# Two interleaved output chains in a seven-product down projection, block sums one per piece, earlier weight sums, and late stores and transposes on another queue

## The chip, the cores and the metric

The kernel runs on one core of a Trainium2 chip. The time is the device time of one launch in microseconds (us). Lower is better. Before the change it is 247.21 us, the median of three runs (245.82 to 247.61).

## The reference

The inputs are q, k and v of shape 4 x 8 x 768 x 64 (batch, heads, sequence, head width). A retention over time feeds a mixer: a low-rank product along the sequence, then a two-layer MLP with relu along the model width of 512 (hidden width 2048, rank 32).

```python
state = gamma * state + einsum('bhd,bhe->bhde', k[:, :, t], v[:, :, t])
y[:, :, t] = scale * einsum('bhd,bhde->bhe', q[:, :, t], state)   # for t = 0 .. 767
x = y.transpose(0, 2, 1, 3).reshape(4, 768, 512)
h = x.transpose(0, 2, 1) @ U @ V                                  # U 768 x 32, V 32 x 768
u = x + h.transpose(0, 2, 1)
out = u + maximum(u @ w_ch1, 0) @ w_ch2
```

## The kernel before

**Tiling.** The four batch elements are called blocks. A block's 768 rows are six chunks of 128. The recurrence is computed by chunks: `score` multiplies a chunk's k and q to 128 x 128 squares per head and VectorE multiplies these by the decay mask (tiles `a`, line 435); `mix` multiplies them with v and adds what the running state gives (bank `o`, line 450), and ScalarE copies the sum to `x`; `state` carries the state on. The low-rank product follows when a block has all six chunks: `lr_proj` (tile `pc`), `lr_expand` with four adds on VectorE into `x` (line 482), and then the transposed copy `uT`, in three pairs of chunks, by TensorE with a copy (`lr_turn_pe`) or by a transposing DMA (`lr_turn`, line 496).

**The MLP of a block.** The up projection is 32 pieces, each with four matmuls into an `mlp` bank: 16 of 512 columns and 16 of 256. A relu takes each bank into `gT`; every third one is on VectorE (line 629), the others are on ScalarE (line 631). Block 0's down projection is direct: 24 pieces of four matmuls. That of blocks 1 to 3 is Strassen's method with Winograd's sums. The 768 rows, the 2048 hidden units and the 512 columns are each cut in halves, and seven products of half-size blocks replace eight. Each product (p1 to p7) is made for three row tiles i of 128 rows, so there are 21 of them, each with eight matmuls of 256 columns. Before them stand sums on VectorE: of the weights, once (`w2_sums`, line 527, tiles `w2t`, four groups of four), and of the hidden values (`g_sums`, lines 535 to 538, tiles `gS`, and one in place in `gT`, four groups of four for each block). Behind them, VectorE takes the banks out: `keep` (line 565: `da` after p1, `db` after p6, `dc` after p7) adds the residual and keeps an intermediate result, `give` (line 571) adds it to the final half row. For one row tile, p1, p6, p7 and p4 are added up in one bank of the ring `A`, with a `keep` between them, p5 and p3 in bank `C`, and p2 is in bank `B`. A product that adds to a bank waits until the `keep` of the product before it in that bank is done, since both use the same bank.

**Stages.** `weave` runs the MLP of one block, with the retention and the low-rank product of the next block set in between at given shares of the MLP's length (the numbers in the tracks at the program's end). Stage k is the MLP of block k with the retention of block k+1; stage 3 has none. Startup and block 0's retention come ahead. In stage 0 and for most of stage 1, GpSimd (POOL) casts and scales what is loaded (line 263).

**What sets the order.** The schedule is manual: instructions are issued in program order, each engine works its own queue in that order, and an instruction waits on semaphores for its inputs and for its buffers. PSUM has eight banks, given out by rings (`RINGS`): `mlp` 0 to 2, `s` 3 and 4, `o` 5, `qk` 6, `st` 7; `A`, `B` and `C` of the down projection share 0, 6, 1 and 2 with these. DMAs are issued on ScalarE's queue (ACT: transposes, stores of blocks 1 to 3) and on SyncE's (SP: loads, block 0's stores).

## Time and profile before

| | |
|---|---|
| median of the runs | 247.21 us |
| the profiled execution: its time | 247.24 us |
| its span in the trace | 245.5 us |
| its mean granted TensorE clock | 0.993 of full speed |
| busy share of TensorE, VectorE, ScalarE, GpSimd | 89%, 60%, 36%, 34% |

The span is what the trace covers; the 1.7 us between it and the time lie around the program. The chain of work that ended last is mostly the seven products, and TensorE's time is mostly the up projection (columns: line, engine, operation, output and inputs, count, then busy time, mean of one in ns, then the idle time just ahead of these and what ended most of it):

```profile
PE 7%; DVE 0%; issue 0%
PE A L552 4%; PE C L552 2%; PE B L552 1%; DVE dc L565 0%; DVE o L571 0%; DVE da L565 0%
...
L624 PE MATMUL mlp<-uT,w1b 128*128 128x512 f16 (+1 forms) x512 | 90.6, 330 | 3.7 <-ACT gT L631 1.3
L435 DVE TENSOR_TENSOR a<-s,mask 128x512 bf16<-128x512 f32 x36 | 23.0, 681 | 7.4 <-PE s L431 7.4
L552 PE MATMUL A<-w2t,gT 128*128 128x256 f16 x144 | 18.6, 272 | 3.0 <-DVE dc L565 1.5
L450 PE MATMUL o<-vd,a 128*128 128x64 bf16 x144 | 8.2, 195 | 5.1 <-DVE a L435 5.0
L552 PE MATMUL A<-w2t,gS 128*128 128x256 f16 x72 | 9.3, 273 | 3.6 <-DVE da L565 3.6
```

The chain is followed back only as far as the trace releases it. The last number of a row says for how long TensorE stood still right ahead of those instructions, and for whom. Names are those of the program, with the buffer's number left out.

### The profile page before, as it was taken

How to read it: one execution, taken by the hardware profiler on the slowest of the kernel's cores; microseconds unless marked ns; L12 is line 12 of the kernel's file. 1: busy time of each engine (PE TensorE's matmuls, PEld its weight loads, DVE VectorE, ACT ScalarE, POOL GpSimd, SP SyncE). 2: the span in 40 equal slices, each digit the busy share in tenths (PEclk: the TensorE clock that was granted, in tenths of full speed). 3: DMA queues.
4: the chain of work that ended last, by engine and by line, in shares of the span. 5: the costliest groups of instructions: out<-in, count | busy, mean ns of one | idle time of the engine just before them, and what ended most of it. 6: DMA issues, size and time to landing. Idle time of an engine off the chain costs nothing. (4 is left out here: it accounts for less than half of the span.)

```text
span 245.5 us, 5333 instructions
## 1 busy us (share of the span) xinstructions
PE 218.7 (89%) x2149; PEld 144.4 (59%) x2152; DVE 146.7 (60%) x289; ACT 87.7 (36%) x175; POOL 83.5 (34%) x121
## 2 busy tenths in 40 slices
PE   7898999999999589967879979999799989998993
PEld 3466444866454335543668663665688745656882
DVE  6676444329796542786475664496955652757442
ACT  3267454554642155634311001665321014541000
POOL 5532988787887571465416100000000000000000
PEclk9999999999999999999799999999999999999999
DMA  6997999999999999999993154422222262000222
GB/s 186 294 288 181 324 328 275 375 268 220 220 195 234 232 240 176 224 189 231 206 166 116 45 128 132 86 47 43 43 45 88 98 158 45 0 0 4 85 85 88
DMA packets 94633, 39.22 MB, mean 160 GB/s; under 512 B 78096, under 2 KB 87312, under 8 KB 94608
## 3 DMA queue, kind: packets, MB, share of 16 engines
q1 hardware_dynamic: 73008, 29.43, 52.0%
q10 hardware_dynamic: 21600, 9.44, 16.3%
q8 instruction: 17, 0.28, 0.5%
q14 instruction: 8, 0.07, 0.1%
HBM read 27.85 MB, written 6.29 MB: 139 GB/s over the span
## 5 line engine op out<-in xcount | busy, mean ns | idle before, releaser
L624 PE MATMUL mlp<-uT,w1b 128*128 128x512 f16 (+1 forms) x512 | 90.6, 330 | 3.7 <-ACT gT L631 1.3
L624 PEld LDWEIGHTS <-w1b 128*128 128x128 f16 x512 | 48.8, 99 | 36.3 <-issue 5.1
L631 ACT ACTIVATE gT<-mlp 128x512 f16<-128x512 f32 (+1 forms) x88 | 43.2, 497 | 63.7 <-PE mlp L624 41.2
L629 DVE TENSOR_SCALAR gT<-mlp 128x256 f16<-128x256 f32 (+1 forms) x40 | 21.4, 536 | 36.9 <-PE mlp L624 36.7
L552 PEld LDWEIGHTS <-gT 128*128 128x128 f16 x288 | 27.5, 98 | 8.2 <-issue 4.6
L435 DVE TENSOR_TENSOR a<-s,mask 128x512 bf16<-128x512 f32 x36 | 23.0, 681 | 7.4 <-PE s L431 7.4
L84 ACT ACTIVATE x<-o 128x512 f16<-128x512 f32 x21 | 12.5, 596 | 37.0 <-PE o L450 24.3
L552 PEld LDWEIGHTS <-gS 128*128 128x128 f16 x216 | 20.6, 98 | 6.7 <-issue 3.9
L659 PE MATMUL mlp<-w2b,gT 128*128 128x512 f16 x96 | 24.2, 380 | 0.0
L263 POOL TENSOR_TENSOR qkd<-in,gq 128x512 bf16<-128x512 f32 x18 | 19.1, 1059 | 13.2 <-DMA in<-in_q_dram 10.2
L263 POOL TENSOR_TENSOR qkd<-in,gk 128x512 bf16<-128x512 f32 x18 | 19.5, 1084 | 8.5 <-DMA in<-in_k_dram 7.9
L552 PE MATMUL A<-w2t,gT 128*128 128x256 f16 x144 | 18.6, 272 | 3.0 <-DVE dc L565 1.5
L84 ACT ACTIVATE state<-st 64x256 bf16<-64x256 f32 x40 | 15.0, 375 | 7.0 <-PE st L328 3.8
L261 POOL CAST vd<-in 128x512 bf16<-128x512 f32 x18 | 11.9, 662 | 15.5 <-issue 9.6
L450 PE MATMUL o<-vd,a 128*128 128x64 bf16 x144 | 8.2, 195 | 5.1 <-DVE a L435 5.0
L552 PE MATMUL A<-w2t,gS 128*128 128x256 f16 x72 | 9.3, 273 | 3.6 <-DVE da L565 3.6
L659 PEld LDWEIGHTS <-gT 128*128 128x128 f16 x96 | 8.2, 98 | 7.2
L177 PE MATMUL mlp<-ones 128*128 128x512 bf16 x32 | 10.2, 448 | 1.8 <-DVE ones L170 1.4
L482 DVE TENSOR_TENSOR x<-s,x 128x256 f16<-128x256 f32 (+1 forms) x16 | 8.2, 552 | 5.8 <-PE qk L478 4.7
L565 DVE TENSOR_TENSOR dc<-A,x 128x256 f32<-128x256 f32 x9 | 3.8, 425 | 11.9 <-PE A L552 11.9
L290 POOL CAST w2b<-in 128x512 f16<-128x512 f32 x16 | 9.8, 613 | 2.3 <-DMA in<-in_moe_w_ch_dram 1.7
L450 PEld LDWEIGHTS <-a 128*128 128x128 bf16 x144 | 6.2, 99 | 6.9 <-DVE a L435 6.4
(110 smaller groups left out, 272.6 us busy)
## 6 DMA issues: line engine op xcount, KB each, us to landing
in<-in_moe_w_ch_dram SPq DMA_DIRECT2D x32, 256.0 KB, 5.7
in<-in_k_dram SPq DMA_DIRECT2D x24, 256.0 KB, 5.3
in<-in_q_dram SPq DMA_DIRECT2D x24, 256.0 KB, 5.5
in<-in_v_dram SPq DMA_DIRECT2D x24, 256.0 KB, 5.4
out_dram<-o ACTq DMA_DIRECT2D x18, 256.0 KB, 2.0
out_dram<-o SPq DMA_DIRECT2D x12, 128.0 KB, 3.7
Vf<-in_moe_V_dram SPq DMA_DIRECT2D x4, 96.0 KB, 4.0
qkT<-qkd ACTq DMA_TRANSPOSE x12, 3.1
```

What stands on the lines that cost most here:

```text
L84: nc.scalar.activation(dst, src, AF.Copy)
L177: nc.tensor.matmul(idle_bank[0], ones[:, :P], ones, start=True, stop=True, skip_group_check=True)
L261: nc.gpsimd.tensor_copy(out=t, in_=src)
L263: nc.gpsimd.tensor_tensor(t, src, g[:, ci, :, None].to_broadcast([P, H, D]), op=ALU.mult)
L290: nc.gpsimd.tensor_copy(out=w2b[:, m], in_=take("w2", m))
L435: nc.vector.tensor_tensor(a, four(sp[i]), causal(mask), op=ALU.mult)
L450: nc.tensor.matmul(o_p[:, ts(h, D)], a[i][:, h // 2], vb[:, h], start=(ci == 0 and h == 0), stop=True, skip_group_check=True)
L552: nc.tensor.matmul(acc[key, i], lhs[:, m, ts(i, P)], rhs[:, m], start=(fresh and m == 0), stop=(m == NH - 1), skip_group_check=True)
L624: nc.tensor.matmul(g_p[:, :sz], w1b[:, c, ts(m, P)], uTs[b][:, ds(j, nj), c], start=(c == 0), stop=(c == NCB - 1))
L629: nc.vector.tensor_relu(gT[:, m, ds(lo, sz)], g_p[:, :sz])
L631: nc.scalar.activation(gT[:, m, ds(lo, sz)], g_p[:, :sz], AF.Relu)
L659: nc.tensor.matmul(ch, gT[:, m, ts(j, P)], w2b[:, m], start=(m == 0), stop=(m == NM - 1))
```

## The change

It has six parts.

1. The 21 products come in a new order. Two row tiles' chains in the ring `A` are begun together: p1, p6 and p7 of tile 0 and tile 1 stand side by side, and other products lie between two of the same chain. The `give` of the lower right quarter now follows whichever of p5 and p7 is later. The intermediate tiles `d` and the masked scores `a` have two buffers each.
2. `g_sums` gives back its four sums as four steps, and these are hung one by one on four pieces in a row (from pieces 12, 16 and 24). Of the last group, two stand behind the last piece of the up projection, one behind p1 of tile 0 and one behind p1 of tile 1.
3. In blocks 1 to 3 every fourth relu is on VectorE, not every third.
4. From stage 1 on, the ring `mlp` has a fourth bank, number 6; the last expansion of the low-rank product takes bank `st` and the transposes on TensorE in stage 1 take bank `o`, both instead of `qk`.
5. The weight sums `w2_sums` stand earlier in stage 0: at 0.47, 0.52, 0.57 and 0.62 of its MLP instead of 0.58, 0.68, 0.78 and 0.88.
6. The stores of the MLP of blocks 2 and 3 and the transposes of block 3 (`qkT` and `uT`) are issued by SyncE instead of ScalarE.

```diff
-             "A": [0, 6], "B": [1], "C": [2]}
+             "A": [6, 0], "B": [1], "C": [2]}
...
     def turn_dma(b, ci):
-        nc.scalar.dma_start_transpose(
+        (nc.sync if b > 2 else nc.scalar).dma_start_transpose(
...
-            a = rmid.tile([P, 4, P], bf16, tag=f"a{i}", name=f"a{i}_{b}_{ci}")
+            a = rmid.tile([P, 4, P], bf16, tag=f"a{i}", bufs=2,
+                          name=f"a{i}_{b}_{ci}")
...
     def lr_turn(b, j):
-        nc.scalar.dma_start_transpose(
+        (nc.sync if b > 2 else nc.scalar).dma_start_transpose(
...
     def g_sums(gT, gS, m):
-        nc.vector.tensor_tensor(s1, a21, a22, op=ALU.add)
-        nc.vector.tensor_tensor(s2, s1, a11, op=ALU.subtract)
-        nc.vector.tensor_tensor(a21, a11, a21, op=ALU.subtract)
-        nc.vector.tensor_tensor(s4, a12, s2, op=ALU.subtract)
+        return [part(nc.vector.tensor_tensor, *x) for x in (
+            (s1, a21, a22, ALU.add), (s2, s1, a11, ALU.subtract),
+            (a21, a11, a21, ALU.subtract), (s4, a12, s2, ALU.subtract))]
...
-            t = outp.tile([P, DQ], fp32, tag=f"d{nm}", bufs=1,
+            t = outp.tile([P, DQ], fp32, tag=f"d{nm}", bufs=2,
...
-                stores.append((nc.scalar, out[b, ts(j, P)], r[0]))
+                stores.append((nc.sync if b > 1 else nc.scalar,
+                               out[b, ts(j, P)], r[0]))
...
+        def c22(i, nm):
+            done.add((nm, i))
+            if ("p5", i) in done and ("p7", i) in done:
+                give("C", i, i + NP, 1, held["c", i])
...
-            order += [(p1, i)] if i == 0 else []
-            order += [(p2, i), (p6, i), (p5, i), (p7, i)]
-            order += [(p1, i + 1)] if i + 1 < NP else []
-            order += [(p4, i), (p3, i)]
+        order = [(p1, 0), (p1, 1), (p2, 0), (p6, 0), (p6, 1), (p5, 0), (p7, 0),
+                 (p7, 1), (p2, 1), (p4, 0), (p3, 0), (p4, 1), (p5, 1), (p1, 2),
+                 (p2, 2), (p6, 2), (p3, 1), (p7, 2), (p5, 2), (p4, 2), (p3, 2)]
...
-                if n[0] % 3 == 0:
+                if n[0] % (3 if b == 0 else 4) == 0:
...
-            for i, at in ((0, 15), (2, 19), (4, 26), (6, len(pieces) - 1)):
-                cost, f = pieces[at]
-                pieces[at] = (cost, chain(f, part(g_sums, gT, gS, i)))
-            return pieces + down_pairs(b, gT, gS)
+            def late(steps, at, fs):
+                for i, f in enumerate(fs):
+                    cost, g = steps[at + i]
+                    steps[at + i] = (cost, chain(g, f))
+            late(pieces, 12, g_sums(gT, gS, 0))
+            late(pieces, 16, g_sums(gT, gS, 2))
+            late(pieces, 24, g_sums(gT, gS, 4))
+            s1, s2, s3, s4 = g_sums(gT, gS, 6)
+            late(pieces, len(pieces) - 1, [chain(s1, s2)])
+            down = down_pairs(b, gT, gS)
+            late(down, 0, [s3, s4])
+            return pieces + down
...
-            first = [part(lr_expand, b - 1, 4, 2),
-                     part(lr_turn_pe if b == 2 else lr_turn, b - 1, 4)]
+            first = [part(lr_expand, b - 1, 4, 2, "st"),
+                     part(lr_turn_pe, 1, 4, "o") if b == 2 else
+                     part(lr_turn, b - 1, 4)]
+            if b == 2:
+                RINGS["mlp"] = [6, 0, 1, 2]
...
-                    tracks.append(([part(w2_sums, m)], 0.58 + 0.05 * m, 1))
+                    tracks.append(([part(w2_sums, m)], 0.47 + 0.025 * m, 1))
```

Three places show what moves. The first is VectorE's queue in stage 0, where block 0's down projection begins. Here `gT` is a relu, `a_1_0` are the masked scores of block 1's chunk 0, `o_0` is the first output add of block 0, and `w2t` are the weight sums. Before:

```order
L629 TENSOR_SCALAR gT_853<-mlp_1078 128x256
L435 TENSOR_TENSOR a_1_0_1144<-s_1134,mask 128x512
L435 TENSOR_TENSOR a_1_0_1146<-s_1135,mask 128x512
L664 TENSOR_TENSOR o_0_1167<-mlp_1096,x_372 128x512
L527 TENSOR_TENSOR w2t_90<-w2b 128x512
L527 TENSOR_TENSOR w2t_91<-w2b,w2t_90 128x512
L527 TENSOR_TENSOR w2t_92<-w2b 128x512
L527 TENSOR_TENSOR w2t_93<-w2b,w2t_91 128x512
```

And after, from the second group of weight sums on (the first group, the same four rows, stands right ahead, behind the last relu):

```order
L528 TENSOR_TENSOR w2t_90<-w2b 128x512
L528 TENSOR_TENSOR w2t_91<-w2b,w2t_90 128x512
L528 TENSOR_TENSOR w2t_92<-w2b 128x512
L528 TENSOR_TENSOR w2t_93<-w2b,w2t_91 128x512
L436 TENSOR_TENSOR a_1_0_1152<-s_1142,mask 128x512
L436 TENSOR_TENSOR a_1_0_1154<-s_1143,mask 128x512
L680 TENSOR_TENSOR o_0_1175<-mlp_1100,x_372 128x512
```

Eight weight sums have moved ahead of chunk 0's masks. The other eight now stand behind that output add and ahead of chunk 1's masks.

The second place is VectorE's queue where the seven products of block 3 begin (`gS` and `gT` from line 505 are sums of hidden values, `da`, `db` and `dc` are the kept results with the row tile's number, `o_0` and `o_3` are output rows). Before:

```order
L629 TENSOR_SCALAR gT_3156<-mlp_3361 128x256
L535 TENSOR_TENSOR gS_3157<-gT_3156 128x768
L536 TENSOR_TENSOR gS_3157<-gS_3157,gT_3156 128x768
L537 TENSOR_TENSOR gT_3156<-gT_3156 128x2x384
L538 TENSOR_TENSOR gS_3157<-gT_3156,gS_3157 128x768
L565 TENSOR_TENSOR da_0_3392<-A_3383,x_2592 128x256
L571 TENSOR_TENSOR o_0_3403<-B_3394,da_0_3392 128x256
L565 TENSOR_TENSOR db_0_3413<-A_3383,x_2592 128x256
L565 TENSOR_TENSOR dc_0_3432<-A_3383,x_2592 128x256
L571 TENSOR_TENSOR o_3_3434<-C_3415,dc_0_3432 128x256
```

And after:

```order
L635 TENSOR_SCALAR gT_3156<-mlp_3373 128x256
L505 TENSOR_TENSOR gS_3157<-gT_3156 128x768
L505 TENSOR_TENSOR gS_3157<-gS_3157,gT_3156 128x768
L565 TENSOR_TENSOR da_0_3390<-A_3381,x_2592 128x256
L505 TENSOR_TENSOR gT_3156<-gT_3156 128x2x384
L565 TENSOR_TENSOR da_1_3402<-A_3393,x_2592 128x256
L505 TENSOR_TENSOR gS_3157<-gT_3156,gS_3157 128x768
L571 TENSOR_TENSOR o_0_3414<-B_3405,da_0_3390 128x256
L565 TENSOR_TENSOR db_0_3424<-A_3381,x_2592 128x256
L565 TENSOR_TENSOR db_1_3434<-A_3393,x_2592 128x256
L565 TENSOR_TENSOR dc_0_3453<-A_3381,x_2592 128x256
L571 TENSOR_TENSOR o_3_3455<-C_3436,dc_0_3453 128x256
```

Two of the last four sums have moved behind `da` of tile 0, and the kept results of tile 1 now stand between those of tile 0.

The third place is ScalarE's queue in stage 2, at chunks 2 and 3 of block 3's retention (`state` is the copy of the running state, `qkT` the transposed q and k of a chunk, `x` the copy of a mixed chunk). Before:

```order
L84 ACTIVATE state_179<-st_2517 64x4x64 x2
L403 DMA_TRANSPOSE qkT_2_2615<-qkd_2_2428 128x8x128
L631 ACTIVATE gT_2448<-mlp_2637 128x512
L631 ACTIVATE gT_2448<-mlp_2643 128x512
L631 ACTIVATE gT_2448<-mlp_2659 128x256
L84 ACTIVATE x_2592<-o_2665 128x512
L631 ACTIVATE gT_2448<-mlp_2679 128x256
```

And after:

```order
L84 ACTIVATE state_179<-st_2517 64x4x64 x2
L637 ACTIVATE gT_2448<-mlp_2618 128x512
L637 ACTIVATE gT_2448<-mlp_2639 128x512
L637 ACTIVATE gT_2448<-mlp_2653 128x256
L637 ACTIVATE gT_2448<-mlp_2659 128x256
L84 ACTIVATE x_2592<-o_2665 128x512
L637 ACTIVATE gT_2448<-mlp_2679 128x256
```

The transposes have gone to SyncE's queue, and one more relu stands between the two copies.

More of the change, by code (lines that the diff above doesn't have):

```diff
@@ L484, in lr_expand, with lr_turn_pe @@
                 xs[b][:, ds(j0, nj), ts(c, P)], op=ALU.add)
-    def lr_turn_pe(b, j0):
-        tp = bank("qk", fp16)
+    def lr_turn_pe(b, j0, tag="qk"):
+        tp = bank(tag, fp16)
         for j in range(j0, j0 + 2):
@@ L603, in p3 @@
             give("C", i, i, 1, held["b", i])
-        order = []
-        for i in range(NP):
-            order += [(p1, i)] if i == 0 else []
-            order += [(p2, i), (p6, i), (p5, i), (p7, i)]
-            order += [(p1, i + 1)] if i + 1 < NP else []
-            order += [(p4, i), (p3, i)]
+        order = [(p1, 0), (p1, 1), (p2, 0), (p6, 0), (p6, 1), (p5, 0), (p7, 0),
+                 (p7, 1), (p2, 1), (p4, 0), (p3, 0), (p4, 1), (p5, 1), (p1, 2),
+                 (p2, 2), (p6, 2), (p3, 1), (p7, 2), (p5, 2), (p4, 2), (p3, 2)]
         return [(0.874, part(f, i)) for f, i in order]
@@ L639, in mlp_pieces, with quad @@
         else:
[L640 removed]
+            gS = gtp.tile([P, 3, NH, TH], fp16, tag="gS", name=f"gS_{b}")
+            def quad(t, i):
                 return [t[i], t[i + 1], t[i + NH], t[i + NH + 1]]
[L643 to L650 removed]
+            def late(steps, at, fs):
+                for i, f in enumerate(fs):
+                    cost, g = steps[at + i]
+                    steps[at + i] = (cost, chain(g, f))
+            for t, i in ((lo, 0), (lo, 2), (hi, 0), (hi, 2), (lo, 4), (hi, 4),
+                         (lo, 6), (hi, 6)):
+                pieces += quad(t, i)
+            late(pieces, 12, g_sums(gT, gS, 0))
[6 more added lines that the diff above has]
+            return pieces + down
         hold = {}
```

9 lines of the change are left out of this document (3 added, 6 removed).

## The prediction

> **What bounds the kernel now.** I read the page's first part, then the busy time by stretches cut where a stage begins. "Stage k" is the MLP of block k woven with the retention of block k+1. The rows below are the page's first line, and then the second half of stage 0 and stages 1 to 3 (columns: stretch, its length, busy time of the engines PE, PEld, DVE, ACT, POOL, granted clock, DMA share, GB/s).
>
> ```profile
> PE 218.7 (89%) x2149; PEld 144.4 (59%) x2152; DVE 146.7 (60%) x289; ACT 87.7 (36%) x175; POOL 83.5 (34%) x121
> 50.70:87.10 36.40, 32.75 (x339) 18.17 (x337) 25.08 (x39) 15.56 (x26) 27.65 (x32) 1.00 1.10 220
> 87.10:148.00 60.90, 50.88 (x488) 35.57 (x488) 37.19 (x69) 18.94 (x40) 23.10 (x26) 0.97 0.90 171
> 148.00:199.40 51.40, 47.70 (x480) 33.81 (x481) 32.85 (x68) 17.32 (x38) 0.00 (x0) 1.00 0.34 78
> 199.40:245.50 46.10, 40.45 (x304) 28.80 (x304) 23.20 (x51) 10.89 (x22) 0.00 (x0) 1.00 0.16 52
> ```
>
> TensorE carries the kernel in every stage. Stages 1 and 2 hold the same MLP and the same retention, yet stage 1 takes 9.5 us more, and only stage 1 has POOL at work (23.1 us). So what can be won or lost is TensorE's waits, which the view of waits lists, TensorE's alone (total, times, longest). Stage 1:
>
> ```profile
> PE o L450 <- DVE a L435: 4.6, 5, 2.2
> PE A L552 <- DVE da L565: 1.5, 1, 1.5
> PE A L552 <- DVE db L565: 0.9, 1, 0.9
> PE mlp L624 <- ACT gT L631: 0.8, 1, 0.8
> PE A L552 <- DVE dc L565: 0.5, 1, 0.5
> PE mlp L624 <- DVE gT L629: 0.4, 1, 0.4
> ```
>
> Stage 2:
>
> ```profile
> PE A L552 <- DVE da L565: 1.4, 1, 1.4
> PE mlp L624 <- ACT gT L631: 0.5, 1, 0.5
> ```
>
> Stage 3:
>
> ```profile
> PE A L552 <- DVE da L565: 0.6, 1, 0.6
> PE A L552 <- ACT gT L631: 0.5, 1, 0.5
> PE mlp L624 <- DVE gT L629: 0.2, 1, 0.2
> ```
>
> And the second half of stage 0:
>
> ```profile
> PE s L478 <- DVE pc L86: 1.1, 1, 1.1
> PE o L450 <- DVE a L435: 0.3, 1, 0.3
> ```
>
> Nearly all are waits for VectorE. One conversion is needed. In the timeline of the end of stage 2, eight-matmul products follow each other at 0.87 us though each is drawn 1.03 us long:
>
> ```profile
> 192.94 1.04 PE L552 MATMUL A<-w2t,gS 128*128 128x256 f16 x8
> 193.81 1.04 PE L552 MATMUL C<-w2t,gS 128*128 128x256 f16 x8
> 195.42 1.03 PE L552 MATMUL A<-w2t,gT 128*128 128x256 f16 x8 [0.57 <-DVE db L565]
> 196.97 1.03 PE L552 MATMUL A<-w2t,gT 128*128 128x256 f16 x8 [0.51 <-DVE dc L565]
> 199.43 0.81 PE L624 MATMUL mlp<-uT,w1b 128*128 128x512 f16 x3 [0.55 <-DVE o L571]
> ```
>
> So a listed wait of 0.51 us delays by 0.68 (196.97 - 195.42 - 0.87): I add 0.16 to each.
>
> **Part 1: w2 sums moved up (stage 0).** In VectorE's queue two groups of four sums now stand ahead of chunk 0's masks, and two ahead of chunk 1's; TensorE's mix waits for the masks. DVE, POOL and TensorE rows from that place of the timeline:
>
> ```profile
> 50.09 0.43 DVE L629 TENSOR_SCALAR gT<-mlp 128x256 f16<-128x256 f32 x1 [0.89 <-PE mlp L624]
> 55.42 0.40 PE L450 MATMUL o<-vd,a 128*128 128x64 bf16 x8
> 56.23 0.57 DVE L527 TENSOR_TENSOR w2t<-w2b 128x512 f16<-128x512 f16 x1
> 56.91 0.42 DVE L527 TENSOR_TENSOR w2t<-w2b,w2t 128x512 f16<-128x512 f16 x1
> 58.33 1.09 POOL L263 TENSOR_TENSOR qkd<-in,gk 128x512 bf16<-128x512 f32 x1
> 58.44 1.26 DVE L527 TENSOR_TENSOR w2t<-w2b,w2t 128x512 f16<-128x512 f16 x1
> 59.62 0.68 DVE L435 TENSOR_TENSOR a<-s,mask 128x512 bf16<-128x512 f32 x1
> 60.88 0.40 PE L450 MATMUL o<-vd,a 128*128 128x64 bf16 x8
> ```
>
> The shortest of these sums takes 0.42 us (56.91); one that meets a POOL instruction ends 0.28 us after it (58.33 + 1.09 = 59.42, the sum at 59.70). A group therefore takes between 4 x 0.42 = 1.7 us and the 3.47 seen here (56.23 to 59.70). POOL is busy 27.65 of 36.4 us in this stretch, so I take 3.1, near the upper end. The queue is free at 50.5 (50.09 + 0.43); two groups last until 56.8, two masks of 0.64 until 58.1. Mix of chunk 0 ran at 55.42 without a wait: it now ends 2.5 us later (bounds 0, since 50.5 + 3.4 + 1.3 = 55.2, and 3.3). Then the block's first output add (0.6) and two groups more, to about 64.6, masks to 65.9; TensorE would reach mix of chunk 1 at 60.88 + 2.5 = 63.4: 2.3 us more (bounds 0 and 3.4). Loss 4.8. What is behind on VectorE (output adds) is waited for by nobody soon. Given back later: the wait for pc, whose cast stood behind the last sums, 1.1 + 0.16 = 1.3, the mask wait 0.3 + 0.16, and some 0.2 of pauses too short for the list: 2.0. **Net +2.8 us.**
>
> **Part 2: stage 1.** Fourth mlp bank: the two mlp waits (0.8 and 0.4, with 0.16 each) go, since a fourth bank buys TensorE about one more piece (0.87 us for four matmuls of 512 columns, as for eight of 256): -1.5. The five mask waits are two pairs and one:
>
> ```profile
> 108.73 0.29 PE L450 MATMUL o<-vd,a 128*128 128x64 bf16 x4 [1.57 <-DVE a L435]
> 117.18 0.29 PE L450 MATMUL o<-vd,a 128*128 128x64 bf16 x4 [2.15 <-DVE a L435]
> 113.72 1.28 DVE L535 TENSOR_TENSOR gS<-gT 128x768 f16<-128x768 f16 x1
> 115.97 0.55 DVE L538 TENSOR_TENSOR gS<-gT,gS 128x768 f16<-128x768 f16 x1
> 117.99 1.90 PE L624 MATMUL mlp<-uT,w1b 128*128 128x256 f16 x8
> 116.70:122.80 6.10, 5.31 (x40) 4.14 (x40) 2.63 (x4) 2.12 (x5) 2.65 (x3) 0.72 1.16 206
> ```
>
> Chunk 1 (108.73): seven of eight sums still stand between its masks and chunk 0's; I leave the wait. Chunk 2 (117.18): its masks stood behind four sums (113.72 to 116.52); now three of these run a piece each earlier, the fourth behind the masks. Gain 2.15 + 0.30 + 2 x 0.16 = 2.75 (bounds: 1.3, if the three meet POOL at 1.28 each, and 2.75). Behind that wait the clock is at 0.72 over 6.1 us (eight matmuls at 117.99 are drawn 1.90 us long, those of the same width above 1.04): (1 - 0.72) x 6.1 = 1.7 us, of which I put 0.25 on pauses: 1.45, gone with the wait. The da wait (1.5 + 0.16): p6 is now the fourth product, 2.6 us behind the up projection; but mix of chunk 3 follows it and its masks stand behind the third and fourth sum, which may meet POOL: I expect 1.2 us there, gain 0.45 (bounds -0.5 and 1.66). Last mask wait: 0.5. **-6.7 us.**
>
> **Part 3: what stays.** The waits for db, dc and o at the end of stages 1 and 2 look like the change's main target. I count nothing for them:
>
> ```profile
> 194.03 0.68 DVE L482 TENSOR_TENSOR x<-st,x 128x512 f16<-128x512 f32 x1
> 194.78 2.65 ACTq L496 DMA_TRANSPOSE uT<-x  x2
> uT<-x ACTq DMA_TRANSPOSE x6, 3.2
> ```
>
> The next stage's first matmul needs the second of two transposes: issued at about 196.1, landing 3.2 later at 199.3; it started at 199.43. Both wait for the expansion's last add (194.71). The expansion is still followed by six products, and the adds by as much, so a faster chain of products only waits longer at 199.43.
>
> **Part 4: stages 2 and 3.** Stage 2: ACT's relu behind two transposes (0.5 + 0.16), one of them now on SyncE; da (1.4 + 0.16), for here POOL is idle and relu, two sums of 0.55 and da end 2.1 us behind the up projection, p6 comes at 2.6. **-2.3 us.** Stage 3: da 0.81, ACT relu 0.63, VectorE relu 0.40, and the last dc, 0.68 (as at 196.97): the new order puts at least one other product between two of a chain, 0.87 us against 0.42 + 0.1 of VectorE. **-2.5 us.** Nothing: stores and transposes on SyncE, whose loads are all issued by then; buffers of two; ACT's extra relus (ACT is busy 17.3 of 51.4 us).
>
> Sum: 2.8 - 6.7 - 2.3 - 2.5 = -8.7. The profiled execution took 247.24 us (span 245.5), the median is 247.21: 247.24 - 8.7 = **238.5 us**.
>
> **Rivals.** (1) Half clock in stage 0. The clock fell after a wait of 2.15 + 0.30 us; the two new waits are as long. Each would cost 1.45 us: 240.0 or 241.4. Against it: the 1.57 us wait at 108.73 did nothing, so the place decides. The Trainium skill (TensorE: Matmul & The Clock Gate, section "What's actually happening") puts the half rate behind at least one idle window of about 3.4 us; by that rule neither new wait would do it and 238.5 stands, but then the drop at 117 should not be there either; the trace goes against the rule taken literally.
>
> (2) Chunk 2's mask wait stays in stage 1, POOL meeting every sum: +2.75 +1.45 = 242.7.
>
> (3) The w2 sums are hidden after all, POOL being paused at 50 to 57: -4.8, 233.7.
>
> (4) Slower: sums spread out meet POOL more often. In stage 1 a sum takes 1.28 us beside POOL (113.72) and 0.55 alone (115.97); if all sixteen meet it where half do now, an estimate by that pair, eight times 0.73 = 5.8 us more stand before relus and masks, and stage 1's 6.7 is lost: 247.24 + 2.8 + 5.8 - 2.3 - 2.5 = 251.0. It decides once the 6.7 is gone and three more sums meet POOL (2.2, above the 2.0 that the other stages leave). Against it: POOL works 23.1 of 60.9 us, so a sum alone is likelier than one that meets it.
>
> (5) SyncE's transposes delay ACT's. Block 3's first four qkT transposes come on SyncE and the first uT transpose of block 2 waits for them. Normally all four land ahead of the expansion's adds; if two were still on their way, one after the other at the 3.2 us above, uT would come 2 x 3.2 = 6.4 later: 244.9. The Trainium skill (DMA: Bandwidth & Descriptors, "Silent corruption: two transposing streams in flight at once") asks for just this wait; no run here shows its price yet.
>
> **The numbers.** Forecast 0.50, rival 1 0.14, rival 2 0.12, rival 3 0.06, rival 4 0.06, rival 5 0.06, several small losses together (243 to 247) 0.06. Between 234.0 and 243.5 lie the forecast with its bounds, rivals 1 and 2, half of rival 3 and the lowest of the small losses: eight in ten. Within 1% is what a measurement of this kernel can't tell from no change. Faster 0.84, same 0.10 (rival 5 and two thirds of the small losses, above 244.7), slower 0.06.
>
> **What would show it.** Right: two mix waits of over 2 us at 55 to 66, no wait for pc, stage 1 some 54 us long at full clock, no da wait in stages 2 and 3, a wait of up to 0.8 us for uT where stages 2 and 3 begin. Wrong: no mix wait in stage 0 (part 1), the wait of chunk 2 still there (part 2), first matmuls of stages 2 and 3 earlier than 7.3 us behind the expansion (part 3).

## The result, and the profile after

The changed kernel takes 239.96 us (median of 4 runs, 239.04 to 243.99) against 247.41 us: a ratio of 0.969, 95% interval 0.964 to 0.975. That is 7.5 us less. The forecast was 8.7 us less, with the range 234.0 to 243.5. Here and below, medians are over all executions, while ratios leave out slow ones, those over 1.5% longer than the fastest of their kernel.

The stretches below are those of the prediction, cut anew where TensorE's first matmul of the next stage starts (columns: stretch, length, busy time of PE, PEld, DVE, ACT and POOL, granted clock, DMA share, GB/s). The first fence is the execution that was profiled with the result; its time was 243.99 us, the highest of the four, so the same kernel was profiled once more (a_again, second fence, 241.82 us). That one, too, was the slowest of its four, so both traces show less of the gain than the medians.

```profile
50.70:92.00 41.30, 35.09 (x341) 18.73 (x339) 25.30 (x39) 15.75 (x26) 30.98 (x37) 0.95 1.13 221
92.00:150.10 58.10, 51.89 (x489) 35.23 (x488) 36.46 (x67) 19.05 (x41) 21.74 (x23) 0.95 1.03 182
150.10:198.80 48.70, 47.04 (x480) 33.81 (x480) 32.26 (x66) 18.46 (x40) 0.00 (x0) 1.00 0.25 61
198.80:242.10 43.30, 39.82 (x304) 28.85 (x304) 22.45 (x49) 11.77 (x24) 0.00 (x0) 0.99 0.21 56
```

```profile
50.70:88.60 37.90, 33.10 (x339) 18.12 (x338) 23.65 (x39) 15.64 (x26) 27.88 (x34) 1.00 1.00 216
88.60:145.20 56.60, 48.81 (x488) 34.39 (x487) 34.62 (x67) 19.19 (x41) 24.18 (x26) 0.99 1.18 205
145.20:196.60 51.40, 49.76 (x480) 34.43 (x480) 32.25 (x66) 18.44 (x40) 0.00 (x0) 0.94 0.23 57
196.60:240.00 43.40, 39.82 (x304) 28.84 (x304) 22.42 (x49) 11.76 (x24) 0.00 (x0) 1.00 0.21 56
```

The lengths before were 36.4, 60.9, 51.4 and 46.1 us. Stage 3 is 2.8 and 2.7 shorter in the two, and that is the whole of what they agree on: stage 0 is 4.9 or 1.5 longer, stage 1 is 2.8 or 4.3 shorter, stage 2 is 2.7 shorter or the same. Much of the difference is the clock. A granted clock of 0.95 over 41.3 us is a loss of 0.05 x 41.3 = 2.1 us, over 58.1 us 2.9; 0.94 over 51.4 us is 3.1. In the first profile the clock fell to half three times while TensorE worked. These three stretches show it:

```profile
67.30:70.70 3.40, 3.40 (x17) 1.16 (x15) 0.82 (x2) 0.41 (x2) 2.58 (x4) 0.50 1.19 216
91.60:95.00 3.40, 3.40 (x17) 1.04 (x16) 1.35 (x3) 0.98 (x2) 2.25 (x3) 0.55 0.92 244
115.40:118.80 3.40, 3.40 (x13) 1.50 (x12) 1.89 (x4) 1.50 (x4) 2.88 (x3) 0.54 1.35 215
```

Each lasts about 3.4 us and so costs 1.7. What TensorE waited for in these executions shows where they come from. The view of waits of the changed kernel (first profile), TensorE alone, for 50 to 70 us, then for the rest of stage 0, then for stage 1 (of the lists of waits, here and below, only the costliest rows are shown):

```profile
PE o L451 <- DVE a L436: 4.2, 4, 2.0
```

```profile
PE qk L491 <- ACT uT L84: 1.1, 1, 1.1
PE qk L491 <- DVE x L483: 0.8, 1, 0.8
```

```profile
PE o L451 <- DVE a L436: 2.9, 4, 1.7
PE mlp L630 <- DMA uT<-x: 1.7, 1, 1.7
PE A L552 <- DVE db L565: 1.1, 1, 1.1
PE mlp L630 <- ACT gT L637: 0.3, 1, 0.3
```

The half clocks at 67, 91 and 115 us follow these: the second mix wait of stage 0, the two waits of the transposes where stage 0 ends, and a mix wait of stage 1. Of the waits that the prediction listed for stage 1, the one for da is gone, and those of the up projection for a relu have shrunk to 0.3. Two kinds are new: two pairs of mix waits in stage 0, as forecast, and 1.7 us for a DMA, uT, at the end of stage 1. The two waits of the transposes are not new: the kernel before has the same two, 1.1 and 0.8 us, and the prediction's list of stage 0 leaves them out. In a_again the wait for uT is longer still:

```profile
PE mlp L630 <- DMA uT<-x: 4.2, 1, 4.2
PE o L451 <- DVE a L436: 2.2, 4, 1.2
```

With those 4.2 us comes the half clock of stage 2 in that profile (0.94 of 51.4 us); it lasts from 144.2 to 151.0 us, 6.8 us and not 3.4.

### The profile page after: what moved, and what is told of

Read it like the earlier page. It is cut to its first block, busy times and chain, and to the rows that moved or that the text cites. A ratio compares the mean times of both kernels' runs of the same rounds, so it can differ in the third digit from the quotient of the medians.

```text
span 242.1 us, 5345 instructions
## 1 busy us (share of the span) xinstructions
PE 221.2 (91%) x2152; PEld 144.8 (60%) x2152; DVE 144.7 (60%) x283; ACT 89.9 (37%) x181; POOL 84.2 (35%) x121
## 4 chain that ended last, share of the span: by engine, by line
PE 65%; DVE 16%; DMA 9%; SPq 3%; issue 2%; ACT 2%; POOL 1%; ACTq 1%; DVEq 0%; POOLq 0%
PE mlp L630 32%; PE A L552 10%; PE mlp L675 6%; DVE w2t L528 5%; PE C L552 4%; DMA in<-in_v_dram 3%; DVE a L436 3%; PE B L552 3%; DVE gS L505 3%; DMA uT<-x 3%; DVE x L483 3%; DMA in<-in_q_dram 2%; SPq L141 2%; PE s L431 2%; PE o L451 2%
## 5 line engine op out<-in xcount | busy, mean ns | idle before, releaser
L630 PEld LDWEIGHTS <-w1b 128*128 128x128 f16 x512 | 48.7, 99 | 35.8 <-issue 5.9
L637 ACT ACTIVATE gT<-mlp 128x512 f16<-128x512 f32 (+1 forms) x94 | 45.6, 490 | 60.6 <-PE mlp L630 47.7
L635 DVE TENSOR_SCALAR gT<-mlp 128x512 f16<-128x512 f32 (+1 forms) x34 | 18.9, 556 | 33.1 <-PE mlp L630 32.9
L675 PE MATMUL mlp<-w2b,gT 128*128 128x512 f16 x96 | 26.0, 402 | 0.0
L261 POOL CAST vd<-in 128x512 bf16<-128x512 f32 x18 | 12.5, 696 | 14.8 <-issue 8.2
L177 PE MATMUL mlp<-ones 128*128 128x512 bf16 x34 | 10.8, 448 | 1.4 <-DVE ones L170 1.4
L290 POOL CAST w2b<-in 128x512 f16<-128x512 f32 x16 | 10.4, 668 | 2.4 <-DMA in<-in_moe_w_ch_dram 1.9
L284 POOL CAST w1b<-in 128x512 f16<-128x512 f32 x16 | 9.5, 615 | 2.5 <-DMA in<-in_moe_w_ch_dram 2.2
L84 ACT ACTIVATE qkT<-qk 128x1024 bf16<-128x1024 bf16 x6 | 6.1, 1024 | 10.3 <-PE qk L395 10.3
```

The source lines that it names most:

```text
L84: nc.scalar.activation(dst, src, AF.Copy)
L261: nc.gpsimd.tensor_copy(out=t, in_=src)
L630: nc.tensor.matmul(g_p[:, :sz], w1b[:, c, ts(m, P)], uTs[b][:, ds(j, nj), c], start=(c == 0), stop=(c == NCB - 1))
L635: nc.vector.tensor_relu(gT[:, m, ds(lo, sz)], g_p[:, :sz])
L637: nc.scalar.activation(gT[:, m, ds(lo, sz)], g_p[:, :sz], AF.Relu)
L675: nc.tensor.matmul(ch, gT[:, m, ts(j, P)], w2b[:, m], start=(m == 0), stop=(m == NM - 1))
```

## The experiments

The times, with ratios to runs of the kernel before on the same chip (95% interval), and the span of each profiled execution. The first four runs share one chip, the next four another, then three, and best2 is alone, so across these groups ratios are compared and not medians:

| run | what it is | median us | ratio | span us |
|---|---|---|---|---|
| a_again | the changed kernel | 240.71 | 0.969 (0.963 to 0.975) | 240.0 |
| w2_late | changed, weight sums at the old place | 238.24 | 0.961 (0.956 to 0.966) | 235.8 |
| w2_only | before, weight sums moved up | 248.60 | 1.004 (1.001 to 1.007) | 246.2 |
| order_only | before, new order of products | 242.91 | 0.979 (0.973 to 0.984) | 241.0 |
| qkt_act | changed, qkT transposes on ScalarE | 239.18 | 0.964 (0.956 to 0.972) | 240.4 |
| tidy | w2_late and qkt_act together | 238.68 | 0.960 (0.950 to 0.969) | 233.7 |
| tidy_early | tidy, retention earlier in stages 1, 2 | 232.15 | 0.938 (0.931 to 0.945) | 229.2 |
| tidy_block | tidy, block sums in fours again | 238.22 | 0.962 (0.955 to 0.969) | 237.5 |
| relu4_only | before, every fourth relu on VectorE | 244.84 | 0.984 (0.977 to 0.992) | 244.9 |
| three_banks | tidy, three banks for the up projection | 237.65 | 0.949 (0.942 to 0.956) | 232.6 |
| best1 | tidy_early, sums and transposes spread | 230.52 | 0.930 (0.926 to 0.935) | 228.7 |
| best2 | best1, p1 of tile 2 earlier | 228.99 | 0.926 (0.923 to 0.929) | 227.3 |

Runs of one kernel spread by up to 6 us (three_banks: 234.40 to 240.59), and the clock is part of it: in the traces an execution holds none, one, two or three half clocks of 1.7 us or more. Between these two runs of three_banks the mean granted clock (1.000 and 0.986) accounts for 3.3 of 6.2 us; the rest is open. So a difference of less than about 2 us is read from waits and stages in the traces here, and not from medians.

**a_again.** No edit.

> The changed kernel once more, for a profile at a higher mean clock than 0.977 and as the neighbour of the next runs. If the two mix waits of stage 0 start the half clock in only some executions, this one has both waits (2.0 to 2.4 us and about 1.9 us between 55 and 66), stage 0 ends near 90.0 instead of 92.0, and the span is near 237.5. If the half clock belongs to the waits, it is there again and the span is near 242.

Stage 0 ended at 88.6 us, both mix waits were there but shorter (2.5 us in all, against 4.2), and no half clock followed in stage 0. So the half clock does not come with the change as such; the last section works out when it comes. The span was 240.0 and not 237.5, for the uT wait of 4.2 us and the half clock with it, which neither expectation had.

**w2_late.** Only the place of the weight sums is taken back.

```diff
-                    tracks.append(([part(w2_sums, m)], 0.47 + 0.025 * m, 1))
+                    tracks.append(([part(w2_sums, m)], 0.58 + 0.05 * m, 1))
```

> The changed kernel with the weight sums back at their old places (0.58 to 0.88 of stage 0). Theory (the prediction's part 1: the early sums cost 2.8 us net, through the masks behind them): no mix wait over 0.5 us in stage 0, the wait for pc is back, first matmul of stage 1 near 87.2, and the time 2.8 us below the changed kernel's, about 237 where that gives 240. Rival A (the early sums cost nothing in the end, since what they free later gives it back): the same time within 0.5 us. Rival B (they help): 1 us or more above it.

The ratios differ by 0.0085, 2.1 us in the direction of the theory, give or take 1.9 by the two intervals. TensorE's waits in the second half of stage 0 are now these:

```profile
PE s L479 <- DVE pc L86: 1.2, 1, 1.2
...
PE o L451 <- DVE a L436: 0.7, 2, 0.4
```

The mix waits fell from 2.5 or 4.2 to 0.7, and the wait for pc is back, as the theory has it. Rival B falls, and rival A is unlikely. The price depends on the execution: stage 0 lasts 37.4 us here, against 41.3 in the first profile with its half clock, but only 37.9 in a_again. Stage 1 begins at 88.1 and not near 87.2 as expected.

**w2_only.** The same numbers, put into the kernel before.

```diff
-                    tracks.append(([part(w2_sums, m)], 0.58 + 0.05 * m, 1))
+                    tracks.append(([part(w2_sums, m)], 0.47 + 0.025 * m, 1))
```

> The kernel before with nothing but the weight sums moved up. Theory: 2.8 us above before, about 250, with mix waits of 2.0 to 2.4 us at chunks 0 and 1 and no wait for pc; up to 1.7 us more where the clock halves behind them. Rival: no change within 0.5 us.

Slower by 0.4% (0.1 to 0.7%): 1.0 us, not 2.8. Stage 0's second half and stage 1:

```profile
50.70:90.00 39.30, 34.13 (x337) 18.66 (x335) 24.85 (x39) 15.24 (x25) 28.59 (x34) 0.96 1.07 215
90.00:148.50 58.50, 49.22 (x488) 34.53 (x487) 35.91 (x69) 18.82 (x39) 22.53 (x25) 1.00 0.92 172
```

In the first of them the mix waits are 2.9 us in all, the longest 2.6. Stage 0 is 2.9 us longer (39.3 against 36.4), of which 0.04 x 39.3 = 1.6 is a half clock: 1.3 are left. TensorE waited for chunk 0's masks alone. Chunk 1's were ready at 65.5 us, later than in a_again (64.3), but the half clock (59.7 to 63.1) had held TensorE up, and it came no sooner. Stage 1, in turn, is 2.4 us shorter than before, 1.7 of it because no half clock came there. That is not shown to be the work of the edit: the mix wait at chunk 2, 2.4 us, is still there, and by their mean granted clocks the runs of w2_only hold as many half clocks as those of the kernel before (mostly 0.993 in the one, 0.986 to 1.000 in the other).

**order_only.** The new table of products and the `give` that follows it, in the kernel before; the d tiles and the masked scores have two buffers, as in the changed kernel.

```diff
...
-            order += [(p2, i), (p6, i), (p5, i), (p7, i)]
-            order += [(p1, i + 1)] if i + 1 < NP else []
-            order += [(p4, i), (p3, i)]
+        order = [(p1, 0), (p1, 1), (p2, 0), (p6, 0), (p6, 1), (p5, 0), (p7, 0),
+                 (p7, 1), (p2, 1), (p4, 0), (p3, 0), (p4, 1), (p5, 1), (p1, 2),
+                 (p2, 2), (p6, 2), (p3, 1), (p7, 2), (p5, 2), (p4, 2), (p3, 2)]
```

> The kernel before with the new order of the 21 products, and two buffers each for the d tiles and the masked scores; sums in groups of four, relus, banks, queues and weight sums as before. Theory (the order is worth only the wait for da and, in stage 3, the last dc, since the ends of stages 1 and 2 wait for uT): stage 3 shorter by about 1.2 us, stages 1 and 2 by 0.5 to 1 each through da, in all 2.0 to 3.0 below before, and the first matmul of stages 2 and 3 still about 4.7 us behind the last add of the expansion. Rival (the interleaved chains shorten the ends of stages 1 and 2 as well, by the listed waits for db, dc and o): 4.5 to 6 us below before, and uT no longer the last.

Faster by 2.1%, 5.2 us. That is the size that the rival gave, but not by its way. TensorE's waits in stage 1, and in stage 2:

```profile
PE o L451 <- DVE a L436: 4.3, 5, 2.6
PE A L553 <- DVE db L566: 1.1, 1, 1.1
PE mlp L630 <- ACT gT L637: 0.7, 1, 0.7
PE mlp L630 <- DMA uT<-x: 0.7, 1, 0.7
```

```profile
PE A L553 <- DVE db L566: 1.1, 1, 1.1
PE mlp L630 <- DMA uT<-x: 0.8, 1, 0.8
```

At the end of stage 2 db and uT together still take 1.9 us, against 0.57 + 0.51 + 0.55 = 1.6 for db, dc and the first matmul of the next stage before. So the ends gained nothing, as the theory says: the first matmuls of stages 2 and 3 start 4.7 and 4.8 us behind the end of the expansion's last add, as before (4.7 both times). Gone in all three stages is the wait for da, 1.5, 1.4 and 0.6 us, even though all four sums of the last group stand ahead of da here. Stage 1 lasts 58.4 us by the trace (60.9 before), stage 2 50.1 (51.4), stage 3 44.5 (46.1): 2.5 + 1.3 + 1.6 = 5.4, less 0.9 in stage 0, which the edit does not touch: there the mix waits are 1.4 us in this execution and 0.3 before, behind weight sums of up to 1.3 us. The theory had the right places and too small a price; the waits for da, with 0.16 each, are 4.0 of the 5.4, and the rest is not told apart.

**qkt_act.** Block 3's qkT transposes go back to ScalarE's queue.

```diff
-        (nc.sync if b > 2 else nc.scalar).dma_start_transpose(
+        nc.scalar.dma_start_transpose(
             out=qkT, in_=qkd.rearrange("p n h d -> p (n h d)"))
```

> The changed kernel with the qkT transposes of block 3 back on ScalarE; uT of block 3 and the stores stay on SyncE. Theory (the four qkT transposes on SyncE run at the end of stage 1 and hold up ScalarE's two uT transposes): uT of block 2 is issued within 0.3 us of the expansion's last add, the wait ahead of stage 2 falls from 1.7 to 4.3 us to about 0.9, and at most 0.7 us comes back in stage 2 as a wait for a relu; 0.5 to 3 us below the changed kernel, 237 to 239.5. Rival (uT waits for the bandwidth of the DMA engines and not for SyncE's transposes): the wait stays at 1.7 us or more, and the time within 0.5 us.

The ratios tell little (0.964 against 0.969, with overlapping intervals). The timeline tells more. At the end of stage 1 of the changed kernel (a_again), SyncE's queue, ScalarE's queue and VectorE (start, length, engine or queue, line, what):

```profile
129.08 9.56 SPq L403 DMA_TRANSPOSE qkT<-qkd  x4
```

```profile
136.33 0.68 DVE L483 TENSOR_TENSOR x<-st,x 128x512 f16<-128x512 f32 x1
```

```profile
140.62 2.64 ACTq L497 DMA_TRANSPOSE uT<-x  x2
```

The last add ends at 137.01, but the first uT transpose is issued at 140.62, 3.6 us later, and 2.0 us behind the end of SyncE's four (129.08 + 9.56 = 138.64). In the first profile the gap is 145.51 - 144.39 = 1.1 us. With qkt_act the two rows are

```profile
142.96 0.68 DVE L483 TENSOR_TENSOR x<-st,x 128x512 f16<-128x512 f32 x1
```

```profile
143.72 2.64 ACTq L497 DMA_TRANSPOSE uT<-x  x2
```

and the gap is 0.08 us. The wait for uT ahead of stage 2 falls to 0.7, so the rival falls: uT itself lands about 3.2 us behind its issue in all these traces, and what was late was the issue. Nothing came back in stage 2, which lasts 48.7 us with SyncE's transposes and without: the wait for a relu that the prediction gave to the transposes on ScalarE stays away with them there. The Trainium skill (DMA: Bandwidth & Descriptors, section "Silent corruption: two transposing streams in flight at once") says that the later of two streams of transposes, from SyncE and from ScalarE, must wait until the earlier one has fully landed; the gap fits that, and its price here was a transpose issued 1.1 and 3.6 us late; what this adds to the kernel's time the ratios do not resolve.

**tidy.** Both edits together.

> The changed kernel with both taken back, the early weight sums and the qkT transposes on SyncE. If the two are independent, the gain of the old place of the weight sums (2.5 us) and that of qkt_act add up: 235.5 to 237.5. If the second only takes the place of the first, 238.

By the ratio (0.960 against 0.961 for w2_late) the second edit adds nothing; by the traces stage 1 takes 54.7 us against 55.9, with the uT wait at 0.7 where it was 1.8. The four runs lie between 235.43 and 240.17, too wide to tell 1.2 us. Left open by the times, then, and settled only for the wait itself. TensorE's waits in stage 1 of tidy:

```profile
PE o L451 <- DVE a L436: 3.2, 4, 1.4
PE A L552 <- DVE db L565: 1.5, 1, 1.5
PE mlp L630 <- DMA uT<-x: 0.7, 1, 0.7
```

**tidy_early.** The retention of blocks 2 and 3 is pulled forward inside stages 1 and 2.

```diff
-                at = [0.06 + 0.11 * i for i in range(NCK)]
+                at = [0.06 + 0.1 * i for i in range(NCK)]
```

> As tidy, with the chunks of the retention in stages 1 and 2 at a spacing of 0.100 of the stage's MLP and not 0.110, so that the expansion comes about 2 us earlier. Theory (the ends of stages 1 and 2 wait for uT, and so for the expansion): no wait for uT where stages 2 and 3 begin, each about 0.7 us or more earlier, 1.0 to 2.5 us below tidy unless new mask waits take it. Rival (the products' own chain bounds the ends): the same time as tidy within 0.5 us.

The ratio falls from 0.960 to 0.938: 5.3 us, over twice what was expected; the two spans, both at full clock, differ by 4.5. TensorE's waits in stage 1:

```profile
PE o L451 <- DVE a L436: 1.2, 3, 0.7
PE A L552 <- DVE da L565: 1.1, 1, 1.1
```

In stage 2 the longest is 0.6 us for da. No wait for uT is left, and none for db. The mix waits of stage 1, 3.2 in tidy, are 1.2 too, because the masks now fall at other places between the sums. Stages 1 and 2 last 50.8 and 47.8 us (tidy: 54.7 and 48.8). So about 2 us of the gain come from the masks and not from an earlier uT, and no run takes the two apart. The first matmuls of stages 2 and 3 now start 5.6 and 5.9 us behind the expansion's last add, where it was 4.7 both times in tidy.

**tidy_block.** Single sums against blocks of four.

```diff
-            late(pieces, 12, g_sums(gT, gS, 0))
-            late(pieces, 16, g_sums(gT, gS, 2))
-            late(pieces, 24, g_sums(gT, gS, 4))
+            late(pieces, 15, [chain(*g_sums(gT, gS, 0))])
+            late(pieces, 19, [chain(*g_sums(gT, gS, 2))])
+            late(pieces, 26, [chain(*g_sums(gT, gS, 4))])
```

> As tidy, with the first three groups of block sums again as blocks of four behind pieces 15, 19 and 26. Theory (part 2: single sums spare chunk 2's masks): a mask wait of 2 us or more at chunk 2 of stage 1 is back, and with it, in some executions, a half clock of 3.4 us; 1.5 to 4 us above tidy. Rival (single sums meet POOL as often and only move the wait to other chunks): within 0.7 us of tidy.

238.22 against 238.68, with ratios of 0.962 and 0.960: the same. The mix wait at chunk 1 doubles (1.2 to 2.4 us), but the wait at chunk 2 does not come back. VectorE's timeline shows why. Here is the third block of sums in the kernel before, and then in tidy_block:

```profile
113.11 0.69 DVE L629 TENSOR_SCALAR gT<-mlp 128x512 f16<-128x512 f32 x1 [2.39 <-PE mlp L624]
113.72 1.28 DVE L535 TENSOR_TENSOR gS<-gT 128x768 f16<-128x768 f16 x1
```

```profile
111.77 0.75 DVE L505 TENSOR_TENSOR gS<-gT 128x768 f16<-128x768 f16 x1
...
113.78 1.39 DVE L505 TENSOR_TENSOR gS<-gT,gS 128x768 f16<-128x768 f16 x1
116.06 1.29 DVE L436 TENSOR_TENSOR a<-s,mask 128x512 bf16<-128x512 f32 x2 [0.88 <-PE s L431]
```

Before, VectorE stood 2.39 us in front of the relu of the piece that the sums hang on, since every third relu is its own and this piece is number 27. The sums do not need that piece (they read what pieces 17 to 24 give), but they stand behind it in the queue. With every fourth relu, VectorE has no relu there: the sums run in that gap, and the masks even wait 0.88 us for TensorE. One caution: in this execution a half clock (111.1 to 114.5 us) brought TensorE to chunk 2 about 1.7 us late. By an estimate from the same rows the masks would otherwise have held it up by some 0.3 us, still far from 2.15; in tidy, at full clock, chunk 2 has no wait either.

**relu4_only.** That reading, alone in the kernel before.

```diff
-                if n[0] % 3 == 0:
+                if n[0] % (3 if b == 0 else 4) == 0:
```

> The kernel before with nothing changed but every fourth relu on VectorE in blocks 1 to 3, where it was every third. Theory (formed on tidy and tidy_block, which spend the same time in stage 1's waits: the relu of piece 26 on VectorE held the third block of sums back, and with it chunk 2's masks): the wait of 2.15 us at chunk 2 is gone, stage 1 is 2 to 2.7 us shorter, 1.7 us more where the half clock goes with it; 243 to 245.5. Rival (the prediction's part 2: single sums remove this wait): the wait is still there, within 0.7 us of before.

244.84 us, within the theory's range: 3.1 us less by the medians, 3.9 by the ratio, 0.984 (0.977 to 0.992). The mix waits of stage 1 are 2.6 us in all where they were 4.6, and VectorE at chunk 2 reads as in tidy_block:

```profile
112.99 0.76 DVE L535 TENSOR_TENSOR gS<-gT 128x768 f16<-128x768 f16 x1
...
117.84 1.29 DVE L435 TENSOR_TENSOR a<-s,mask 128x512 bf16<-128x512 f32 x2 [1.43 <-PE s L431]
```

The wait at chunk 2 is gone; what is left is chunk 1's, 2.1 us. The execution shown is the slowest of the four, with half clocks over 10.2 us, 6.8 of them at 110.0 to 116.8, right ahead of chunk 2. By the same kind of estimate a wait of some 0.3 us is hidden by that. It is also why stage 1 is only 1.0 us shorter in this trace (59.9 us); counted at full clock it is 0.93 x 59.9 = 55.7 against 0.97 x 60.9 = 59.1, 3.4 us shorter. So the relu's share alone is enough to remove the wait. That single sums alone would do it, with every third relu kept, was not tried.

**three_banks.** Without the fourth bank of the up projection.

```diff
-            if b == 2:
-                RINGS["mlp"] = [6, 0, 1, 2]
```

> As tidy, with three banks in the ring of the up projection in all stages. Theory (the prediction's parts 2 and 4: the fourth bank removes the waits of up projection matmuls for a relu): waits of matmuls of the up projection for a relu are back, 1.0 us or more in stage 1 and 0.4 to 0.7 us in stages 2 and 3 each, 1.5 to 3 us above tidy. Rival (the relus' new share removed them): less than 0.5 us above tidy, none of these waits over 0.3 us.

A ratio of 0.949 (from two executions) against 0.960 for tidy: not slower. No matmul of the up projection waits for a relu in any stage's list of waits, with three banks as with four. Stage 2 lasts 50.0 us against 48.8, with one wait of 0.5 us for a relu, ahead of the first product; the rest is in pauses too short for the list. So the theory falls for stage 1, where the prediction counted 1.5 us on the bank, and in stage 2 there is a cost of 1.2 us in one trace. What did remove the waits is not shown: relu4_only, with three banks and the new share of relus, still lists 0.6 us of them in stage 1.

**best1.** What the traces above pointed to: weight sums where VectorE has nothing waiting behind it, and two banks for the two groups of transposes at the end of stage 0.

```diff
-                RINGS["mlp"] = [6, 0, 1, 2]
+                RINGS["mlp"].append(6)
...
-                for m in range(0, NH, 2):
-                    tracks.append(([part(w2_sums, m)], 0.58 + 0.05 * m, 1))
+                for m, w in ((0, 0.54), (2, 0.638)):
+                    tracks.append(([part(w2_sums, m)], w, 1))
...
+                if b == 2:
+                    for m, w in ((4, 0.09), (6, 0.15)):
+                        tracks.append(([part(w2_sums, m)], w, 1))
...
-                tracks.append(([part(lr_turn_pe, b, 0), part(lr_turn_pe, b, 2)],
+                tracks.append(([part(lr_turn_pe, b, 0, "o"), part(lr_turn_pe, b, 2)],
```

> As tidy_early, with two groups of weight sums right behind the masks of chunks 0 and 1 of stage 0 and two in stage 1 (at 0.09 and 0.15), bank o for the first of the two groups of transposes at the end of stage 0, and the fourth bank of the up projection appended behind the other three. Theory (VectorE's queue is free at these places, and the one bank for two groups of transposes costs 1.27 us): no wait for pc over 0.3 us in stage 0, no 1.27 us between the two groups, stage 0 shorter by 2 to 3 us; 229 to 230.5. Rival (what is behind takes it: the sums delay masks in stage 1, the transposes wait for the adds): within 0.7 us of tidy_early, 232.

230.52 us. Stage 0 is 3.0 us shorter in the trace than in tidy_early (its next stage starts at 84.5, not 87.5): the wait for pc, 1.7 us there, is gone, and the waits of the transposes, 1.9, are down to 0.5, with 0.7 where stage 1 begins; but stage 1 is 1.5 us longer, 0.9 of it a wait for a relu of VectorE that eight weight sums in a row hold back. By the ratios (0.930 against 0.938) the gain is 2.0 us; the time is at the edge of the theory's range.

**best2.** The weight sums of stage 1 singly (`w2_steps` gives the four sums of a group as four steps), and p1 of tile 2 ahead of the expansion.

```diff
-                 (p7, 1), (p2, 1), (p4, 0), (p3, 0), (p4, 1), (p5, 1), (p1, 2),
-                 (p2, 2), (p6, 2), (p3, 1), (p7, 2), (p5, 2), (p4, 2), (p3, 2)]
+                 (p7, 1), (p2, 1), (p4, 0), (p3, 0), (p1, 2), (p4, 1), (p5, 1),
+                 (p6, 2), (p2, 2), (p3, 1), (p7, 2), (p5, 2), (p4, 2), (p3, 2)]
...
-                    for m, w in ((4, 0.09), (6, 0.15)):
-                        tracks.append(([part(w2_sums, m)], w, 1))
+                    for m, w in ((4, 0.08), (6, 0.14)):
+                        tracks.append((w2_steps(m), w, w + 0.06))
```

> As best1, with the eight weight sums of stage 1 hung singly between 0.08 and 0.20, and p1 of tile 2 two products earlier, so that its kept result da stands ahead of the expansion's adds, and p6 of tile 2 needs no wait for it. Theory (at the new place of the expansion the adds hold da back, 1.1 us in stage 1 and about 0.6 in stage 2; and eight sums in a row held a relu back by 0.9 us): these three waits go or halve, 1 to 2 us below best1, 228.5 to 229.5. Rival (uT bounds the ends of the stages again, or p7 waits for db instead): the same time as best1 within 0.7 us, with a wait for uT or db of 0.7 us or more.

228.99 us (227.29 to 229.87, 6 runs), 18.1 below the kernel before in the same comparison (247.09), and within the theory's range. Against best1 the ratios, 0.926 and 0.930, give 1.1 us, with overlapping intervals. No wait for da is left in the list from 80 us on. TensorE's three costliest waits from 80 us to the end (total, times, longest):

```profile
PE o L451 <- DVE a L436: 1.0, 4, 0.3
PE o L491 <- DVE x L483: 0.7, 3, 0.3
PE mlp L632 <- ACT uT L84: 0.7, 1, 0.7
```

None lasts as long as 1 us, and the granted clock is 1.00 in every stage of this execution.

## Why the prediction came out right

The time lay in the range and 1.5 us above the forecast. The parts were not all right, and errors of both signs cancelled, so the closeness is in part luck. In a_again, stages 1 and 2 fall 4.7 us short of the forecast gain (4.3 and 0.0 against 6.7 and 2.3), with 3.5 us more of waiting for uT than tidy has and a half clock worth 3.1 us behind it, neither of them in the sum; the early sums cost 1.3 us less than forecast there. Of the signs that the prediction set, no wait for pc and no da wait in stages 2 and 3 came true; a stage 1 of 54 us at full clock (58.1 and 56.6) and a uT wait of at most 0.8 us (1.7 and 4.2 ahead of stage 2) did not.

- **Part 1, +2.8 us: right mechanism, sized for its worse case.** The masks of chunk 0 ran at 57.2 to 58.4 us in the first profile (forecast 56.8 to 58.1), and the loss of 4.8 us is what that profile shows: 4.2 by the list and 0.16 for each of four waits. But it was 3.1 in a_again, where the same sixteen sums met POOL less (chunk 1's masks began at 63.0 us and not at 64.8), and 3.2 in w2_only, where a half clock hid chunk 1's part. Taken back alone, the early sums are worth 2.1 us (give or take 1.9); added alone, they cost 1.0 (0.2 to 1.8).
- **Part 2, -6.7 us: the sum of stage 1 is about right, its terms are not.** With the wait for uT down to 0.7, the trace gives -6.2 (tidy, 54.7). Chunk 2's wait did go, and the half clock behind it; in the first profile one came at 115 us, behind chunk 1's wait. But the step "now three of these run a piece each earlier, the fourth behind the masks" failed: blocks of four do as well (tidy_block), and relu4_only removes the wait alone. It was the relu ahead of the sums. I had read the sums as the cause, since they stood in front of the masks, and had not asked what the sums themselves waited behind. The step "a fourth bank buys TensorE about one more piece" failed too, for stage 1 (three_banks). That da's wait would turn into a mix wait at chunk 3 held, as a size: 1.2 us forecast, 1.2 the longest mix wait of a_again.
- **Part 3, nothing: right,** shown by order_only (the ends unchanged by a faster chain); tidy_early fits (uT no longer waited for once the expansion is earlier). Its last sentence, that a faster chain only waits longer at uT, is what the list of waits of order_only shows.
- **Part 4, -2.3 and -2.5 us: right in size,** -2.7 in stage 2 of the first profile and -2.8 and -2.7 in stage 3. In stage 2 the reason for 0.66 of it was wrong: qkt_act has the transposes back on ScalarE and not the wait. The two terms there, 0.66 and 1.56, add up to 2.2 and not 2.3, and a wait for db of 1.1 us, where 0.6 was, is not among them.
- **"Nothing: stores and transposes on SyncE": wrong.** In the traces this is, with the half clocks, the largest thing that the sum lacks; that it alone made the forecast too low is not shown, since the times with it taken back (qkt_act, tidy) do not stand clear of those without. Rival 5 named the mechanism, priced it at 6.4 us and gave it 6 in 100. It is there in all three profiles with the edit, at 1.1, 3.6 and (w2_late) 1.2 us. In SyncE's queue only the last loads stand ahead of the transposes, and they are issued in the last third of stage 1 (from 129.1 us in a_again, 135.7 in the first profile), while on ScalarE they had come at their marks in stage 2. I had looked at what the transposes no longer hold up, and not at when they would now run. The stores were not tried alone.
- **Rival 1 came in some executions:** behind the second mix wait of stage 0 (first profile), 1.7 us where 1.45 was forecast, and behind the first in qkt_act, but not in a_again, whose waits are shorter. Two more half clocks, at 91 and 115 us of the first profile, were not foreseen. "The place decides" was right; the last section says which place.

## What to carry to other kernels

When an instruction is late, ask of the one ahead of it in its queue what *that* one waits for: here a relu that waited for its matmul held up sums that were ready, and masks behind them. When DMAs are moved to a queue that is empty, work out when they will now start, and with what of their own kind they meet; "off the busy engine" is not the same as free. And when a chain of transfers bounds the end of a stage, speeding up the work beside it gains nothing; starting the chain earlier, with one number changed, gained 4.5 us between two traces here, part of it because masks moved as well.

## What was not expected of the hardware

The clock falls to half for 3.4 us at a time (67.3 to 70.7 us and the two others above), twice for 6.8 (a_again, 144.2 to 151.0, and relu4_only, 110.0 to 116.8), a cost of 1.7 us for each 3.4. It does so behind waits that are shorter than that: 1.6 and 0.3 us at chunk 1 of stage 0 in the first profile were enough, while 2.0 and 0.3 us at chunk 0 of the same stage were not. Where the wait falls decides, and the traces show how. In each of the 14 traces, all changes of the clock lie whole multiples of 3.413 us apart (the first profile's falls: twice 23.9 us, seven times 3.413). Cut into such windows, the two places look like this (columns as in the first fence), chunk 0 in the first two rows and chunk 1 in the third; the window behind the third is the half clock at 67.3 us, shown further up:

```profile
53.67:57.08 3.41, 2.18 (x16) 0.88 (x16) 3.31 (x4) 0.54 (x2) 3.29 (x5) 1.00 0.91 198
57.08:60.50 3.42, 2.31 (x23) 1.44 (x24) 3.32 (x7) 0.98 (x2) 2.91 (x4) 1.00 1.24 229
63.91:67.32 3.41, 1.55 (x18) 0.92 (x17) 2.78 (x4) 1.77 (x3) 3.04 (x4) 1.00 0.97 216
```

A boundary splits chunk 0's waits into 1.23 and 1.11 us of standing still; chunk 1's lie in one window, 1.86. Of the 916 full-clock windows of the 14 traces, TensorE stood still for 1.86 us or more in 14, and a half clock followed each of these; it stood still for 1.84 us or less in all the others, and none followed. The windows lie differently in each execution, so one wait starts a half clock in one and not in another: the same two waits of the transposes, 1.1 and 0.8 us where stage 0 ends, did so in the first profile and not in a_again. The Trainium skill (TensorE: Matmul & The Clock Gate, section "What's actually happening") asks for an idle window of about 3.4 us; the traces here show the half clock behind less, 1.86 us of one window. The spread of several us between runs of one kernel goes in part with the number of such stretches, and in the trace of best2, with no wait of 1 us from 80 us on, there is none while TensorE works.
